# Postponing weight-conversion steps at the start of row 1, and two reorderings around it, in a fused attention and mixer kernel

## The chip, the cores and the metric

The kernel runs on one core of one Trainium2 chip. The metric is the device time of one launch in microseconds (us). A core has five instruction streams that matter here: TensorE (PE, matrix multiplication, with its weight loads as PEld), VectorE (DVE), ScalarE (ACT), GpSimd (POOL) and SyncE (SP, which here only issues DMA transfers). The streams run side by side and wait for each other through semaphores.

## The reference

The first half is attention over 8 batch rows, 8 heads, 576 tokens and a head width of 64, in which scores more than `tau` below the row's maximum are dropped. The second half is one mixer block on the joined heads.

```python
scores = scale * np.matmul(q, k.transpose(0, 1, 3, 2))
thresh = np.max(scores, axis=-1, keepdims=True) - tau
scores = np.where(scores >= thresh, scores, -1000000000.0)
attn = softmax(scores)
x = np.matmul(attn, v)               # then heads side by side: (8, 576, 512)
h = np.maximum(xt @ w_tok1, 0.0) @ w_tok2         # over tokens, xt = x transposed
u = x + h.transpose(0, 2, 1)
h2 = np.maximum(u @ w_ch1, 0.0) @ w_ch2           # over channels, 512 -> 1536 -> 512
return (u + h2)
```

(`softmax` stands for the reference's lines that subtract the maximum, take the exponential and divide by the sum.) The four mixer weights reach the kernel as 64-bit integers that hold float64 bit patterns. The kernel turns them into float32 itself, and that is what this change is about.

## The kernel before

**Units.** Attention is cut into 144 units, 18 to each batch row: two pairs of heads at a time, and a tile of 128 query rows. The main loop (L648) goes over `u`; row 0 is units 0 to 17, row 1 is units 18 to 35. One turn of the loop issues, for unit u, `scores(u)` (TensorE, L306), then the row maximum `mx` (VectorE, L311) and `bias` (GpSimd, L312), and `weigh(u)` on ScalarE: `e` from the scores (L321), then the exponential (L328). It also issues `norm(u-1)` (GpSimd, L339), and for unit w = u-2 the transposition of `e`. Row 0 transposes on TensorE in thirds (`turn`, L357, copied out at L359). Later rows use a VectorE block transpose (`turn_blocks`, L369), and after every third unit that is followed by 16 transfers `eT<-T` issued by SyncE (L378). Every three units `values` (L413, L418) multiplies by v, and the result is copied into `xT`: at L425 by VectorE in row 0, at L423 by ScalarE later. In row 0 these copies are first put in the queue `copies`, which the loop empties a little later. A unit of row 0 in which `values` runs is called a visit: units 5, 8, 11, 14 and 17.

Each engine takes its instructions in the order in which this loop issues them. From row 1 on the score tiles have two PSUM buffers and one unit fills both, so `scores(u+1)` on TensorE has to wait until L321 of `weigh(u)` has read them.

**Filling.** The mixer's work for a finished row is a list `todo` of steps with costs in us. `fill(share)` takes steps from it against a quota per unit. In row 1 a unit calls it with 0.4 ahead of `turn_blocks` and three times with 0.2 inside `weigh`. For row 0 the list is made in unit 20: the token layers (L456, L466, with their VectorE additions L470), then for each group of 256 tokens twelve steps `ch1` of the first channel layer (L509, copied out on ScalarE at L510) and eight steps `ch2` of the second (L530): two halves of 128 tokens (t) by four parts of the weights (part). These steps take their PSUM tile from `ps_mm`, which has two buffers.

**Weight conversion.** The weights are 31 pieces, from 0 to 30. Raw pieces are loaded into a ring of four slots by SyncE (L186). The conversion is a chain of numbered steps k, three for a piece i: k = 3i + part.

- Part 0: GpSimd finishes piece i-1 (L225), SyncE issues the load of piece i+3 into the slot that this frees, and VectorE does L211 for piece i.
- Part 1: ScalarE does L201 for piece i+1, which is the first instruction to read that piece's load, and VectorE does L213 for piece i.
- Part 2: ScalarE does L203 for piece i+1, and VectorE does L217 for piece i.

`weight(n)` issues the next n steps, `weight_to(x)` goes on to step x, and `need(i)` issues whatever is missing for piece i. In row 0 the loop keeps to int(2.25 (u-1)) steps by the end of unit u, so 36 at the end of unit 17. In row 1 a unit has three places for steps, called slots here: slot 1 after `norm`, slot 2 after `turn_blocks` and ahead of `weigh`, slot 3 at the end, after `weigh`. In units 18 and 19, in which row 0's last units still wait to be transposed, `turns_left` is true: slot 1 is empty, `weigh` comes early in the unit, and slot 2 stands after it.

Of the kernel before, what the change touches and what calls it, by code (L numbers as in the profile page):

```python
# [9 lines left out]
F32 = mybir.dt.float32  # L10
# [7 lines left out]
P = 128  # L18
# [3 lines left out]
def kernel(  # L22
# [38 lines left out]
    NCC = DM // P  # L61
# [16 lines left out]
    ps_mm = None  # L78
# [118 lines left out]
    def on_scalar(i, part):  # L197
        if wide(i):
            lo, hi, h2 = raws[i]
            if part == 0:  # L200
                nc.scalar.activation(out=lo.bitcast(I32), in_=lo, func=AF.Copy, scale=2.0**-29)  # L201
            else:
                nc.scalar.activation(out=h2, in_=hi.bitcast(F32), func=AF.Abs)  # L203
# [17 lines left out]
    def on_gpsimd(i):  # L221
        if i >= 0:
            dst = pieces[i][0]
            if wide(i):
                nc.gpsimd.tensor_tensor(out=dst.bitcast(I32), in0=dst.bitcast(I32), in1=raws.pop(i)[0].bitcast(I32), op=ALU.add)  # L225
            else:
                nc.gpsimd.tensor_copy(out=dst, in_=raws.pop(i))
# [5 lines left out]
    def weight(n):  # L233

        nonlocal steps_done
        for k in range(steps_done, min(steps_done + n, 3 * len(pieces) + 1)):
            i, part = divmod(k, 3)
            if part == 0:
                on_gpsimd(i - 1)
                if i:  # L240
                    load_piece(i - 1 + NRAW)
            else:
                on_scalar(i + 1, part - 1)
            on_vector(i, part)
            steps_done = k + 1

    def weight_to(x):

        weight(max(int(x) - steps_done, 0))

    def need(i):

        weight(3 * i + 4 - steps_done)
# [27 lines left out]
    def in_blocks(b):  # L281
        return b > 0
# [32 lines left out]
    def weigh(u):  # L315
        sc, bias = st.pop(u)
        rs = small.tile([P, 2], F32, tag="rs", name=f"rs_{u}")
        e = work.tile([P, 2 * S], F32, tag="e", bufs=3, name=f"e_{u}")
        for h in range(2):
            eh = e[:, S * h : S * h + S].rearrange("p (f x) -> p f x", f=2)  # L320
            nc.scalar.activation(out=eh, in_=sc[h][:, :, 0:HS], func=AF.Prelu, bias=bias[:, h : h + 1], scale=SCALE, alpha=STEEP)  # L321
        st[u] = e, rs

        if b_now:
            fill(0.2)
        for h in range(2):
            eh = e[:, S * h : S * h + S]
            nc.scalar.activation(out=eh, in_=eh, func=AF.Exp, bias=ntau, accum_out=rs[:, h : h + 1])  # L328
            if b_now:
                fill(0.2)  # L330
# [153 lines left out]
    def channel_mlp(b, uT, i):  # L484

        s = {}
        n = min(GR, 2 * S - GR * i)
        nt = n // P

        def turn_u():  # L490

            us, ut = s["us"], s["ut"]
            nc.vector.transpose(
                out=us[:, 0:nt].rearrange("q n a (c d) -> q c (n a) d", c=NCC),
                in_=uT[:, :, GR * i : GR * i + n].rearrange("q c (m r) -> q c m r", r=32),
            )

            def move(a, k):
                nc.sync.dma_start(out=ut[32 * a : 32 * a + 32, 0:nt, k, :], in_=us[32 * k : 32 * k + 32, 0:nt, a, :])

            moves.extend([lambda a=a, k=k: move(a, k) for a in range(4) for k in range(4)])

        def ch1(j):
            need(7 + j)
            if j == 0:
                s["g"] = work.tile([P, NJ, GR], F32, tag="g", bufs=1, name=f"g_{b}_{i}")
            ps = ps_mm.tile([P, GR], F32, tag="mm", name=f"c1_{b}_{i}_{j}")[:, 0:n]
            for c in range(NCC):
                nc.tensor.matmul(ps, lhsT=wc1[:, j, c, :], rhs=uT[:, c, GR * i : GR * i + n], start=(c == 0), stop=(c == NCC - 1))  # L509
            nc.scalar.activation(out=s["g"][:, j, 0:n], in_=ps, func=AF.Relu)  # L510
            if j == 1:
                s["us"] = work.tile([P, GR // P, 4, NCC * 32], F32, tag="us", bufs=1, name=f"us_{b}_{i}")
                if b:
                    s["ut"] = work.tile([P, GR // P, 4, NCC * 32], F32, tag="ut", bufs=1, name=f"ut_{b}_{i}")
                    turn_u()

        def ch2(t, part):
            need(7 + NJ + 3 * part + 2)
            t0 = GR * i + P * t
            if part == 0:  # L520
                s["ps"] = ps_mm.tile([P, NCC, P], F32, tag="mm", name=f"c2_{b}_{i}_{t}")
            ps = s["ps"]
            flat = ps.rearrange("q c d -> q (c d)")
            if part == 0 and not b:
                for c in range(NCC):
                    nc.tensor.matmul(
                        ps[:, c, :], lhsT=uT[:, c, t0 : t0 + P], rhs=ident, is_transpose=True, start=(c == 0), stop=False, skip_group_check=True
                    )
            for j in range(3 * part, 3 * part + 3):
                nc.tensor.matmul(  # L530
                    flat,
                    lhsT=s["g"][:, j, P * t : P * t + P],
                    rhs=wc2[:, j, :],
                    start=(j == 0 and b > 0),
                    stop=(j == NJ - 1),
                    skip_group_check=True,
                )
            if part == 3:
                o = s["us"][:, t].rearrange("q a x -> q (a x)")
                if b:  # L540
                    move_u()
                    nc.vector.tensor_add(  # L542
                        out=o.rearrange("q (c k d) -> q c k d", c=NCC, k=4),
                        in0=ps.rearrange("q c (k d) -> q c k d", k=4),
                        in1=s["ut"][:, t].rearrange("q k (c d) -> q c k d", c=NCC),
                    )
                else:
                    nc.vector.tensor_copy(out=o, in_=flat)
                nc.sync.dma_start(out=out[b : b + 2].rearrange("b s d -> (b s) d")[t0 : t0 + P, :], in_=o)

        def ch2_last(half):

            t0 = GR * i
            w = DM // 2
            ps = ps_mm.tile([P, w], F32, tag="mm", name=f"c2_{b}_{i}_h{half}")
            for j in range(NJ):
                nc.tensor.matmul(  # L557
                    ps, lhsT=s["g"][:, j, 0:P], rhs=wc2[:, j, w * half : w * half + w], start=(j == 0), stop=(j == NJ - 1)
                )
            if half == 0:  # L560
                move_u()
            o = s["us"][:, half].rearrange("q a x -> q (a x)")[:, 0:w]
            cs = slice(NCC // 2 * half, NCC // 2 * half + NCC // 2)
            nc.vector.tensor_add(
                out=o.rearrange("q (c k d) -> q c k d", c=NCC // 2, k=4),
                in0=ps.rearrange("q (c k d) -> q c k d", c=NCC // 2, k=4),
                in1=s["ut"][:, 0].rearrange("q k (c d) -> q c k d", c=NCC)[:, cs],
            )
            nc.sync.dma_start(out=out[b : b + 2].rearrange("b s d -> (b s) d")[t0 : t0 + P, w * half : w * half + w], in_=o)

        if b == B - 2 and n == P:
            return [(0.0067 * n, lambda j=j: ch1(j)) for j in range(NJ)] + [(5.2, lambda half=half: ch2_last(half)) for half in range(2)]
        return [(0.0067 * n, lambda j=j: ch1(j)) for j in range(NJ)] + [
            (2.6 if part or b else 3.0, lambda t=t, part=part: ch2(t, part)) for t in range(nt) for part in range(4)
        ]

    def move_u():
        while moves:
            moves.popleft()()
# [68 lines left out]
    for u in range(len(units) + LAG + 4):  # L648
        on = u < len(units)
        if u == UB:  # L650
            late.close()
            ps_mm = ctx.enter_context(tc.tile_pool(name="ps_mm", bufs=2, space=bass.MemoryType.PSUM))
        if on:
            b_now, p0, t = units[u]
# [6 lines left out]
        last = False  # L661
        visit = False
        if due and not in_blocks(due[0][1]):
            visit = due[0][0] <= u
            last = values_due(u)
# [6 lines left out]
        turns_left = b_now and back and not in_blocks(units[w][0])  # L672
        if b_now:
            if turns_left:
                weigh(u)
            else:
                weight(2)
        else:


            weight_to(2.25 * (u - (1 if visit else 1.5)))
            if visit:
                weigh(u)
        while copies:
            copies.popleft()()
        if last and u < UB:
# [15 lines left out]
        if back and in_blocks(wb):  # L702
            turn_blocks(w)
        if b_now:
            weight(4 if turns_left else 2)
        if turns_left:
            fill(0.6)
        elif on and (b_now or not visit):
# [62 lines left out]
```

## Time and profile before

| | |
|---|---|
| time, median of 3 | 1351.52 us (1350.7 to 1352.07) |
| span of the profiled run | 1349.9 us |
| PE busy, 0 to 100 us | 81.77 of 100.00 us |
| PE busy, 100 to 190 us | 78.78 of 90.00 us |
| PE busy, 190 us to the end | 1146.08 of 1159.90 us |
| VectorE busy, 0 to 100 and 100 to 190 us | 74.95 and 76.72 us |

Row 0's scores run to about 90 us, the conversion ends at about 188 us, and the rest is almost solid TensorE work. In a list of the timeline a line gives the start, the duration, the engine, the line of code, the operation with its output and input, how many instructions are merged into it, and in brackets how long the engine had been idle before it and what it waited for.

### The profile page before, as it was taken

How to read it: one execution, taken by the hardware profiler on the slowest of the kernel's cores; microseconds unless marked ns; L12 is line 12 of the kernel's file. 1: busy time of each engine (PE TensorE's matmuls, PEld its weight loads, DVE VectorE, ACT ScalarE, POOL GpSimd, SP SyncE). 2: the span in 40 equal slices, each digit the busy share in tenths (PEclk: the TensorE clock that was granted, in tenths of full speed). 3: DMA queues.
4: the chain of work that ended last, by engine and by line, in shares of the span. 5: the costliest groups of instructions: out<-in, count | busy, mean ns of one | idle time of the engine just before them, and what ended most of it. 6: DMA issues, size and time to landing. Idle time of an engine off the chain costs nothing.

```text
span 1349.9 us, 17890 instructions
## 1 busy us (share of the span) xinstructions
PE 1306.6 (97%) x6186; PEld 817.1 (61%) x6186; DVE 592.2 (44%) x1026; ACT 585.1 (43%) x1299; POOL 352.5 (26%) x683
## 2 busy tenths in 40 slices
PE   7888899999999999999999999999999999999999
PEld 5565556547474666655665567565656566575677
DVE  6878874445443435434334445434443454201000
ACT  6777654444445435443434444354333454120110
POOL 4565652222222213222222222222221222100000
PEclk8998999999999999999999999999999999999999
DMA  5535764535353544543345435535443453400000
GB/s 123 120 87 127 199 168 97 127 94 136 83 133 89 114 109 96 126 109 88 86 107 125 98 85 123 125 82 115 109 102 83 114 118 79 112 22 17 23 24 32
DMA packets 296746, 135.31 MB, mean 100 GB/s; under 512 B 204816, under 2 KB 289552, under 8 KB 296656
## 3 DMA queue, kind: packets, MB, share of 16 engines
q1 hardware_dynamic: 168944, 118.27, 34.4%
q10 hardware_dynamic: 127712, 15.90, 7.4%
q8 instruction: 49, 0.80, 0.3%
q14 instruction: 41, 0.34, 0.1%
HBM read 43.25 MB, written 9.44 MB: 39 GB/s over the span
## 4 chain that ended last, share of the span: by engine, by line
PE 86%; DVE 6%; DMA 3%; ACT 2%; SPq 1%; issue 1%; POOL 1%; ACTq 0%; DVEq 0%; POOLq 0%
PE c L530 26%; PE c L509 26%; PE sc L306 11%; PE pv L418 9%; PE t L456 5%; PE t L466 4%; PE pv L413 3%; DVE mx L311 2%; PE tx L449 1%; DMA lk<-in_k_dram 1%; ACT e L321 1%; SPq L378 1%; PE c_h L557 1%; DVE T L369 1%; DVE high L211 1%
## 5 line engine op out<-in xcount | busy, mean ns | idle before, releaser
L509 PE MATMUL c<-xT,wc 128*128 128x256 f32 (+1 forms) x1920 | 400.1, 362 | 0.1
L311 DVE TENSOR_REDUCE mx<-sc 128x1 f32<-128x576 f32 x288 | 204.4, 750 | 444.3 <-PE sc L306 443.2
L530 PE MATMUL c<-wc,g 128*128 128x512 f32 x840 | 379.0, 597 | 0.0
L509 PEld LDWEIGHTS c<-xT,wc 128*128 128x128 f32 x1920 | 334.9, 191 | 69.3 <-issue 29.7
L312 POOL TENSOR_SCALAR bias<-mx,toff 128x1 f32<-128x1 f32 x288 | 81.1, 282 | 775.6 <-DVE mx L311 722.7
L321 ACT ACTIVATE e<-sc,bias 128x576 f32<-128x576 f32 x288 | 199.8, 739 | 182.5 <-POOL bias L312 176.7
L530 PEld LDWEIGHTS c<-wc,g 128*128 128x128 f32 x840 | 154.7, 190 | 176.1 <-issue 172.4
L328 ACT ACTIVATE e<-e,ntau 128x576 f32<-128x576 f32 x288 | 221.1, 771 | 0.0
L339 POOL TENSOR_SCALAR e<-e,rr 128x576 f32<-128x576 f32 x288 | 214.3, 756 | 14.8 <-ACT g L510 2.6
L510 ACT ACTIVATE g<-c 128x256 f32<-128x256 f32 (+1 forms) x240 | 86.7, 361 | 296.5 <-PE c L509 283.4
L306 PE MATMUL sc<-kT,qT 64*128 64x288 f32 (+1 forms) x1280 | 190.3, 433 | 6.9 <-ACT e L321 5.9
L369 DVE STREAM_TRANSPOSE T<-e 128x1152 f32<-128x1152 f32 x126 | 171.9, 1364 | 5.5 <-DMA eT<-T 2.9
L306 PEld LDWEIGHTS sc<-kT,qT 64*128 64x128 f32 (+1 forms) x1280 | 105.2, 178 | 92.2 <-issue 57.2
L418 PE MATMUL pv<-eT,lv 128*64 128x384 f32 (+1 forms) x1024 | 136.8, 408 | 0.0
L418 PEld LDWEIGHTS pv<-eT,lv 128*64 128x64 f32 x1024 | 76.9, 138 | 49.9 <-issue 42.1
L423 ACT COPY xT<-pv 128x384 f32<-128x384 f32 (+1 forms) x56 | 21.0, 400 | 164.6 <-PE pv L418 159.5
L466 PE MATMUL t<-w,a 128*128 128x288 f32 x256 | 75.2, 421 | 8.2 <-DVE xT L470 4.8
L542 DVE TENSOR_TENSOR us<-c,ut 128x512 f32<-128x512 f32 x26 | 17.9, 690 | 137.5 <-PE c L530 122.7
L456 PE MATMUL t<-x_sb,w 128*128 128x512 f32 (+1 forms) x180 | 72.4, 549 | 0.0
L466 PEld LDWEIGHTS t<-w,a 128*128 128x128 f32 x256 | 45.9, 192 | 30.2 <-issue 10.5
L470 DVE TENSOR_TENSOR xT<-xT,t 128x288 f32<-128x288 f32 x64 | 28.3, 446 | 70.6 <-PE t L466 69.9
L328 ACT ACTIVATION_READ_ACCUMULATOR e<-e,ntau 128x1 f32 x288 | 56.7, 197 | 0.0
(51 smaller groups left out, 571.2 us busy)
## 6 DMA issues: line engine op xcount, KB each, us to landing
eT<-T SPq DMA_DIRECT2D x672, 108.0 KB, 2.3
scratch<-in_moe_w_ch_dram SPq DMA_DIRECT2D x24, 512.0 KB, 3.7
lv<-in_v_dram SPq DMA_DIRECT2D x32, 288.0 KB, 3.5
out_dram<-us SPq DMA_DIRECT2D x35, 256.0 KB, 2.2
lk<-in_k_dram ACTq DMA_DIRECT2D x109, 72.0 KB, 2.7
lq<-in_q_dram ACTq DMA_DIRECT2D x106, 72.0 KB, 2.3
ut<-us SPq DMA_DIRECT2D x192, 32.0 KB, 1.9
lk<-in_k_dram SPq DMA_DIRECT2D x19, 72.0 KB, 3.2
```

What stands on the lines that cost most here:

```text
L306: nc.tensor.matmul(sc[h][rows, f, 0:HS], lhsT=qT[r, cols], rhs=kT[r, HS * f : HS * f + HS], start=True, stop=True)
L311: nc.vector.tensor_reduce(out=mx[:, c], in_=sc[h][:, :, 0:HS], axis=AX.XY, op=ALU.max)
L321: nc.scalar.activation(out=eh, in_=sc[h][:, :, 0:HS], func=AF.Prelu, bias=bias[:, h : h + 1], scale=SCALE, alpha=STEEP)
L328: nc.scalar.activation(out=eh, in_=eh, func=AF.Exp, bias=ntau, accum_out=rs[:, h : h + 1])
L339: nc.gpsimd.tensor_scalar(out=eh, in0=eh, scalar1=rr[:, h : h + 1], scalar2=1.0, op0=ALU.mult, op1=ALU.mult)
L369: nc.vector.transpose(out=T[:, :, place, :].rearrange("p a (c x) -> p c a x", c=NK), in_=e.rearrange("p (c a x) -> p c a x", c=NK, a=4))
L418: nc.tensor.matmul(to[r], lhsT=lv[:, j, :], rhs=e[j], start=False, stop=(c == NI - 1), skip_group_check=True)
L456: nc.tensor.matmul(to, lhsT=w1[:, t, P * m : P * m + P], rhs=x_sb[:, t, cols], start=(t == 0), stop=(t == NT - 1))
L466: nc.tensor.matmul(to, lhsT=a[:, m, P * c : P * c + P], rhs=w2[:, m, HS * f : HS * f + HS], start=(m == 0), stop=(m == NTK - 1))
L509: nc.tensor.matmul(ps, lhsT=wc1[:, j, c, :], rhs=uT[:, c, GR * i : GR * i + n], start=(c == 0), stop=(c == NCC - 1))
L510: nc.scalar.activation(out=s["g"][:, j, 0:n], in_=ps, func=AF.Relu)
L530: nc.tensor.matmul(flat, lhsT=s["g"][:, j, P * t : P * t + P], rhs=wc2[:, j, :], start=(j == 0 and b > 0), stop=(j == NJ - 1), skip_group_ ...
```

## The change

Three edits. In units 18 and 19, slot 2 issues no steps where it issued four, so the chain is eight steps further back from there on; nothing is left out, and the later slots go on with two steps each until step 93 is done. The eight `ch2` steps of the first token group are taken by part of the weights first (part 0 of both halves, then part 1 of both, and so on), so that the later weights are called for later; both `ps_mm` buffers are then held through the group, so each half keeps its own tile. In the visits of row 0, the steps no longer stand between `norm` and the copies, but at the end of the unit, where the call of `weight_to` that is already there picks them up.

```diff
             if part == 0:
-                s["ps"] = ps_mm.tile([P, NCC, P], F32, tag="mm", name=f"c2_{b}_{i}_{t}")
-            ps = s["ps"]
+                s[t] = ps_mm.tile([P, NCC, P], F32, tag="mm", name=f"c2_{b}_{i}_{t}")
+            ps = s[t]
...
+        last = [(t, part) for t in range(nt) for part in range(4)]
+        if b == 0 and i == 0:
+            last.sort(key=lambda x: x[1])
         return [(0.0067 * n, lambda j=j: ch1(j)) for j in range(NJ)] + [
-            (2.6 if part or b else 3.0, lambda t=t, part=part: ch2(t, part)) for t in range(nt) for part in range(4)
+            (2.6 if part or b else 3.0, lambda t=t, part=part: ch2(t, part)) for t, part in last
         ]
...
-            weight_to(2.25 * (u - (1 if visit else 1.5)))
             if visit:
                 weigh(u)
+            else:
+                weight_to(2.25 * (u - 1.5))
...
         if b_now:
-            weight(4 if turns_left else 2)
+            weight(0 if turns_left else 2)
```

## The prediction

> **What bounds the kernel now.** I read PE's busy row and PEclk in the page's 40 slices first.
>
> ```profile
> PE   7888899999999999999999999999999999999999
> DVE  6878874445443435434334445434443454201000
> PEclk8998999999999999999999999999999999999999
> ```
>
> A slice is 33.7 us. From the sixth on PE is full; its idle time lies in the first five, where VectorE is as busy. After 190 us PE is busy 1146.08 of 1159.90 us, so a shift reached there is carried to the end. What counts is PE's idle time before that. Next, PE's timeline in units 19 and 20:
>
> ```profile
> 106.10 0.82 PE L357 MATMUL tr<-ident,e 128*128 128x128 f32 x6
> 111.28 0.90 PE L357 MATMUL tr<-ident,e 128*128 128x128 f32 x3 [4.37 <-DVE eT L359]
> 112.11 2.29 PE L306 MATMUL sc<-kT,qT 64*128 64x288 f32 x8
> 114.34 1.55 PE L413 MATMUL pv<-eT,vl 128*64 128x384 f32 x4
> 115.67 3.74 PE L418 MATMUL pv<-eT,lv 128*64 128x384 f32 x16
> 119.34 3.18 PE L466 MATMUL t<-w,a 128*128 128x288 f32 x12
> ```
>
> PE stands 4.37 us for a VectorE copy and is slow afterwards: scores take 2.29 us, against 1.24 at 98.53. VectorE meanwhile:
>
> ```profile
> 104.17 0.60 DVE L211 TENSOR_SCALAR high<-high 128x512 f32<-128x512 f32 x1
> ...
> 106.87 0.74 DVE L211 TENSOR_SCALAR high<-high 128x512 f32<-128x512 f32 x1 [0.92 <-ACT high L203]
> ...
> 108.72 1.42 DVE L311 TENSOR_REDUCE mx<-sc 128x1 f32<-128x576 f32 x2
> ...
> 110.69 0.54 DVE L359 COPY eT<-tr 128x384 f32<-128x384 f32 x1
> ```
>
> Unit 19's scores were ready at 105.1, but six steps of unit 18 stand ahead of its maximum and the copy. That is what the change attacks. Last, SyncE's and ScalarE's timelines, for where else the steps are held:
>
> ```profile
> 140.53 0.33 SPq L186 DMA_DIRECT2D scratch<-in_moe_w_ch_dram  x1
> 140.90 10.55 SPq L378 DMA_DIRECT2D eT<-T  x16
> 151.57 16.15 SPq L186 DMA_DIRECT2D scratch<-in_moe_w_ch_dram  x6
> ```
>
> ```profile
> 146.32 0.70 ACT L203 ACTIVATE high<-scratch 128x512 f32<-128x512 f32 x1
> 146.93 1.35 ACT L321 ACTIVATE e<-sc,bias 128x576 f32<-128x576 f32 x2
> ...
> 155.41 0.69 ACT L201 ACTIVATE scratch<-scratch 128x512 int32<-128x512 uint32 x1 [5.08 <-DMA scratch<-in_moe_w_ch_dram]
> ```
>
> The sixteen `eT<-T` of unit 22 hold SyncE for 10.55 us. The load behind them starts at 151.57, and L201 has waited for it 5.08 us. That wait lies behind unit 23's L321, in slot 3.
>
> [...] after the 4.37 us, granted clock 0.50 from 112 to 116. [...] So a waiting L201 holds every L321 behind it; the lines above agree. [...] L211 takes 0.41 us alone and 1.52 at 131.90 beside L225.
>
> **Visits (edit 3).** In units 8 and 17 the steps delay the copies that PE waits for. In unit 17 they run from 95.06 to 97.0, while pv ended at 95.54; PE starts at 97.68 and could at about 96.1: 1.5 us won. In unit 8 0.76 us of steps make 0.6. In units 5, 11 and 14 the steps now run inside VectorE's wait for pv (0.99, 2.31 and 1.68 us idle) and cost nothing; moved behind the copies they push the next maximum by steps less idle time there: about 0.3, 0.4 (part of 0.86 hidden) and 0.1. Sum **-1.3 us** (minus is earlier).
>
> **Eight steps fewer (edit 1), units 18 to 20.** Two steps remain of six. VectorE is through at 105.2, the maximum ends at 106.6, the addition L470 (0.44), `norm`'s pair (0.3) and the copy (0.54) bring PE's next transposition to 107.8: idle 0.9 instead of 4.37, so -3.5. The clock stays up: the scores save 1.05, pv 1.55 (3.45 instead of 5.0). L466 starts at about 113.1 instead of 119.34: **-6.2**.
>
> **Units 20 to 22.** Six steps per unit as before, but in another phase: slot 1 now holds L213 and L217 (1.13 us) instead of L211 and L213 (0.85), and slot 3 holds L211 behind a L203 that follows `weigh`. Against that, L211 and L213 meet L225 less often. I take **+1.0**; between -2 and +2 is possible.
>
> **The wait that moves.** Count steps. Unit 22 starts at step 60 before, at 52 after, as 36 + 2 + 2 + 6 + 6. Its `eT<-T` stand between slots 1 and 2. The first load behind them is issued before with step 63 (piece 24) and read by L201 in step 70: unit 23's slot 3, behind `weigh(23)`. After, it is issued with step 54 (piece 21) and read in step 61: slot 2, **ahead of** `weigh(23)`. Queued behind that L201 are unit 23's L321 and exponentials; `scores(24)` waits for L321, and all PE work behind it too. From the end of the T transposition of unit 22 (140.0 in before's time): 0.1 + 10.55 + 3.65 for landing (151.57 to 155.2) + 0.6 for L201 + 0.7 for the first L321 = 15.6 us. PE's work ahead of `scores(24)` ends at 149.4, or 9.4 after that transposition. So it idles about 6.4 us[...] and runs at half clock, 2.3 us lost (scores 1.05, first layers 1.25). The old wait at this place, 1.82 us at 159.48, goes: **+6.9**.
>
> Unit 25 has the same pattern: step 72 loads piece 27 behind the sixteen transfers, and step 79 reads it in unit 26's slot 2. Before, it was step 81 and step 88 in slot 3, where ScalarE waits 6.20 us but PE only 0.94. PE's work between T and `scores(27)` runs from 165.6 to 174.1, or 8.5 us; the chain is 15.6 again; with half clock for about 2 us, less 0.94 and some waiting that `scores` had inside its rows: **+7.7**. Unit 28's sixteen are followed by no load.
>
> **The second layer's order (edit 2).** Steps reach 88 by the end of unit 27 and 94 in unit 28. By weights, part 2 (needs 85) comes around unit 30, part 3 (94) after it: `need` adds nothing, and the copies L548 hide behind PE. The eight late steps load VectorE in unit 28: **+0.5**, at most 2.
>
> Sum: -1.3 - 6.2 + 1.0 + 6.9 + 7.7 + 0.5 = +8.6; 1351.5 + 8.6 = **1360 us**.
>
> **Rivals.**
> - Faster: the waits that move cost PE no more than the old ones, because a load comes sooner or PE has work left. For it: PE bridged 5.08 and 6.20 us on ScalarE with 1.82 and 0.94 idle. Against: these stood behind L321. -1.3 - 6.2 + 1.0 + 0.5 = -6.0: 1345.5 us.
> - About the same: only one of the two moved waits costs PE its full size; -6.0 + 6.9 = +0.9: 1352.4 us.
> - Slower still: the clock stays halved for 6 us, as from 111 to 117, and unit 28 costs 2 us: 8.6 + 2 x 1.6 + 1.5 = 13.3: 1365 us.
>
> **Chances.** Forecast 0.55, slower still 0.08, the same 0.12, faster 0.25. The limit of 0.2% is 2.7 us, and the case around 1352.4 spreads over it a little on both sides: faster 0.26, same 0.09, slower 0.65. The range, 1344.5 to 1364, takes in the faster rival and the unknown half-clock times, and leaves out the slowest case and a stray tail.
>
> **What would show it.** Right: PE's 4.37 us before L357 shrinks to about 1; L201 waits some 8 us for its load twice, each time just ahead of a L321; PE's `scores` wait over 5 us for L321 near 150 and 175; half clock behind both. Wrong: L201's long waits still follow the exponentials, or `scores` never waits over 3 us there; then the gain of 6 us stands.

## The result, and the profile after

The changed kernel takes 1362.53 us, the median of 6 runs (1360.37 to 1364.71), against 1352.44 for the kernel before in the same session. The ratio is 1.0075, with a 95% interval of 1.006 to 1.0089: 10.1 us slower. The profiled run has a span of 1360.1 us.

The busy row of PE and the granted clock, from the page of the changed kernel:

```profile
PE   7888879999999999999999999999999999999999
...
PEclk8999889999999999999999999999999999999999
```

A slice is 34.0 us. Against the kernel before, the fourth slice has won a tenth of clock, the fifth (136 to 170 us) has lost one, and the sixth (170 to 204 us) has lost a tenth of clock and two of busy time. PE's timeline says where. A number in brackets is the time that PE stood still ahead of the line, and what it waited for:

```profile
106.90 0.55 PE L357 MATMUL tr<-ident,e 128*128 128x128 f32 x3 [1.83 <-DVE eT L359]
107.38 1.24 PE L306 MATMUL sc<-kT,qT 64*128 64x288 f32 x8
...
112.20 3.18 PE L466 MATMUL t<-w,a 128*128 128x288 f32 x12
...
136.48 1.24 PE L306 MATMUL sc<-kT,qT 64*128 64x288 f32 x8
137.65 5.45 PE L509 MATMUL c<-xT,wc 128*128 128x256 f32 x24
149.30 2.92 PE L306 MATMUL sc<-kT,qT 64*128 64x288 f32 x8 [6.20 <-ACT e L321]
152.14 5.83 PE L509 MATMUL c<-xT,wc 128*128 128x256 f32 x16
...
161.28 1.24 PE L306 MATMUL sc<-kT,qT 64*128 64x288 f32 x8
...
182.05 2.92 PE L306 MATMUL sc<-kT,qT 64*128 64x288 f32 x8 [6.97 <-ACT e L321]
...
195.57 1.24 PE L306 MATMUL sc<-kT,qT 64*128 64x288 f32 x8
```

The same stretch in the kernel before, from unit 23's scores on:

```profile
142.84 1.24 PE L306 MATMUL sc<-kT,qT 64*128 64x288 f32 x8
144.01 5.45 PE L509 MATMUL c<-xT,wc 128*128 128x256 f32 x24
149.39 1.24 PE L306 MATMUL sc<-kT,qT 64*128 64x288 f32 x8
150.56 3.72 PE L509 MATMUL c<-xT,wc 128*128 128x256 f32 x16
...
159.48 1.86 PE L306 MATMUL sc<-kT,qT 64*128 64x288 f32 x8 [1.82 <-ACT e L321]
...
185.45 1.87 PE L306 MATMUL sc<-kT,qT 64*128 64x288 f32 x8 [0.94 <-ACT e L321]
```

Unit 19 has won what the change was made for. The wait of 4.37 us is 1.83, the scores behind it take 1.24 us at a granted clock of 1.00 (107 to 110 us), and L466 starts at 112.20 instead of 119.34. At unit 23's scores (136.48, before 142.84) the kernel is still 6.4 us ahead. Then unit 24's scores wait 6.20 us for L321 and unit 27's 6.97. Unit 28's start at 195.57, where before they started at 185.45: 10.1 us behind. After that the distance hardly changes: unit 40's scores start at 281.41 and 272.14, 9.3 us apart, and the last unit's at 1158.78 and 1148.55, 10.2 us apart.

ScalarE's timeline shows what L321 waits for, and SyncE's why the load is late:

```profile
147.97 0.65 ACT L201 ACTIVATE scratch<-scratch 128x512 int32<-128x512 uint32 x1 [7.90 <-DMA scratch<-in_moe_w_ch_dram]
148.52 1.36 ACT L321 ACTIVATE e<-sc,bias 128x576 f32<-128x576 f32 x2
...
180.72 0.65 ACT L201 ACTIVATE scratch<-scratch 128x512 int32<-128x512 uint32 x1 [8.54 <-DMA scratch<-in_moe_w_ch_dram]
181.28 1.35 ACT L321 ACTIVATE e<-sc,bias 128x576 f32<-128x576 f32 x2
```

```profile
133.52 10.43 SPq L378 DMA_DIRECT2D eT<-T  x16
144.06 17.10 SPq L186 DMA_DIRECT2D scratch<-in_moe_w_ch_dram  x6
166.67 10.31 SPq L378 DMA_DIRECT2D eT<-T  x16
177.10 1.01 SPq L186 DMA_DIRECT2D scratch<-in_moe_w_ch_dram  x2
```

Both times the load is issued when the sixteen transfers are out (144.06, 177.10), lands 3.82 and 3.54 us later, and L201 and at once L321 follow it. The waiting L201 holds L321: unit 23's `bias` starts at 139.50 and takes 0.27 us, and L321, which needs it, starts at 148.52. In the kernel before, unit 24's starts at 152.83 and its L321 at 158.69, behind the L201 that waited 5.08 us and the steps after it. Before, the L201 that waited stood behind the exponentials; here it stands directly ahead of L321, so the order in the queue is what has changed.

One rival has to be looked at here. At the first place the chain of waits names GpSimd's L225 as what released the load: it ends at 144.05, and the transfers are out at 143.95. But this L225 belongs to step 60. The one that frees the slot for this load belongs to step 54 and runs at 133.28 for 1.28 us, and in e4_load_ahead below, where nothing stands ahead of it on SyncE, the load of step 54 is issued at 135.01. So it is the transfers that hold it. At the second place the chain itself runs through all sixteen of them.

### The profile page after: what moved, and what is told of

It is laid out like the page before. It is cut to its first block, busy times and chain, and to the rows that moved or that the text cites. A ratio compares the mean times of both kernels' runs of the same rounds, so it can differ in the third digit from the quotient of the medians.

```text
span 1360.1 us, 17887 instructions
## 1 busy us (share of the span) xinstructions
PE 1309.0 (96%) x6186; PEld 818.6 (60%) x6186; DVE 587.5 (43%) x1026; ACT 585.6 (43%) x1299; POOL 353.5 (26%) x683
## 4 chain that ended last, share of the span: by engine, by line
PE 86%; DVE 5%; ACT 3%; DMA 2%; SPq 1%; POOL 1%; issue 1%; ACTq 0%; DVEq 0%; POOLq 0%
PE c L509 26%; PE c L530 26%; PE sc L306 11%; PE pv L418 9%; PE t L456 5%; PE t L466 4%; PE pv L413 3%; DVE mx L311 2%; SPq L378 1%; PE tx L449 1%; DMA lk<-in_k_dram 1%; ACT e L321 1%; PE c_h L557 1%; PE tr L357 1%; ACT e L328 1%
## 5 line engine op out<-in xcount | busy, mean ns | idle before, releaser
L509 PE MATMUL c<-xT,wc 128*128 128x256 f32 (+1 forms) x1920 | 402.7, 364 | 0.1
L509 PEld LDWEIGHTS c<-xT,wc 128*128 128x128 f32 x1920 | 336.5, 192 | 70.7 <-issue 29.7
L321 ACT ACTIVATE e<-sc,bias 128x576 f32<-128x576 f32 x288 | 200.0, 740 | 186.4 <-POOL bias L312 183.9
L418 PE MATMUL pv<-eT,lv 128*64 128x384 f32 (+1 forms) x1024 | 136.3, 406 | 0.0
L418 PEld LDWEIGHTS pv<-eT,lv 128*64 128x64 f32 x1024 | 76.2, 137 | 48.4 <-issue 38.9
L466 PE MATMUL t<-w,a 128*128 128x288 f32 x256 | 74.9, 418 | 8.6 <-DVE xT L470 5.2
L466 PEld LDWEIGHTS t<-w,a 128*128 128x128 f32 x256 | 45.3, 190 | 30.8 <-issue 10.5
```

The lines of the kernel that those rows point to most:

```text
L418: nc.tensor.matmul(to[r], lhsT=lv[:, j, :], rhs=e[j], start=False, stop=(c == NI - 1), skip_group_check=True)
L466: nc.tensor.matmul(to, lhsT=a[:, m, P * c : P * c + P], rhs=w2[:, m, HS * f : HS * f + HS], start=(m == 0), stop=(m == NTK - 1))
```

## The experiments

The question was whether the loss comes from the place of those reads in the count of six steps per unit, or from something else that the change does: the larger backlog itself, the new order of the second layer, or the steps moved in the visits. All ratios are to the kernel before, run beside it on the same chip.

### The three edits one at a time

```diff
# e1_steps_only: the kernel before, with
-            weight(4 if turns_left else 2)
+            weight(0 if turns_left else 2)
# e2_order_only: the kernel before, with a tile for each half, s[t], and
+            last.sort(key=lambda x: x[1])
# e3_visits_only: the kernel before, with
-            weight_to(2.25 * (u - (1 if visit else 1.5)))
             if visit:
                 weigh(u)
+            else:
+                weight_to(2.25 * (u - 1.5))
```

> Only the eight steps fewer; copies and second layer as before. Theory (the first load behind the sixteen transfers is now read ahead of weigh): both long waits of scores for L321 stand as in the changed kernel, 6 to 7 us each, and the visits' gain of 1 to 2 us is missing: about 1364 us, ratio 1.008 to 1.010. Rival (the second layer's order, holding both PSUM buffers, is what costs): the gain of units 18 to 20 remains alone, about 1346 us, ratio 0.995.

Measured: 1363.76 us, ratio 1.0088 (1.0074 to 1.0103). The scores wait 5.39 and 7.02 us for L321. So this edit alone makes the loss; what the two others add or save is within the intervals.

> Only the second layer by weights. Theory: the order moves no wait, within 1 us of before (1351.5 to 1353.5). Rival (the order is what costs): 1357 us or more.

Measured: 1352.66 us, ratio 1.0003 (0.9995 to 1.0011): no difference. Beside the backlog the order may have a use: e1_steps_only, without it, shows two waits in PE's timeline that the changed kernel doesn't have, for GpSimd's last step on the late pieces, 1.7 us in all. In the medians this can't be told from noise:

```profile
202.37 1.13 PE L530 MATMUL c<-wc,g 128*128 128x512 f32 x2 [0.37 <-POOL wc L225]
204.80 1.12 PE L530 MATMUL c<-wc,g 128*128 128x512 f32 x2 [1.30 <-POOL wc L225]
```

> Only the steps behind the copies in the visits. Theory: PE's wait for the copies L425 in units 8 and 17 shrinks from 1.25 and 1.66 us to under 0.5; 1 to 2 us faster than before: about 1351. Rival (the steps behind the copies delay the next maximum and cost more than they save): 1353 to 1356.

Measured: 1351.21 us, ratio 0.9992 (0.9984 to 1.0): about 1 us, at the edge of what the interval can tell. Its PE timeline in units 8 and 17 has the wait that was to shrink, from 1.25 and 1.66 us to 0.34 both times:

```profile
46.62 0.92 PE L357 MATMUL tr<-ident,e 128*128 128x128 f32 x6 [0.34 <-DVE xT L425]
...
96.14 0.92 PE L357 MATMUL tr<-ident,e 128*128 128x128 f32 x6 [0.34 <-DVE xT L425]
```

### The size of the backlog against the place in the count

If backlog costs, fewer steps left out must cost less. If the place costs, three steps in slot 2 (a backlog of two) must do what none does (a backlog of eight), for in both the first load behind the transfers is issued in a unit's slot 2 (with step 60 and with step 54, both multiples of six) and read in the next unit's slot 2, ahead of `weigh`.

```diff
# the changed kernel, with n = 3, 2 or 1
-            weight(0 if turns_left else 2)
+            weight(n if turns_left else 2)
```

> The changed kernel with three steps instead of none in slot 2 of units 18 and 19: only two steps of backlog instead of eight, but the same place in the count of six. Step 60 issues the first load behind the sixteen transfers, step 67 reads it in unit 23's slot 2, ahead of weigh. Theory (place counts): both waits of scores for L321 stand, over 5 us each, and most of the gain at unit 19 is gone: 1360 to 1368 us. Rival (backlog counts): within 2 us of before, 1350 to 1354.

> The same with two steps instead of none: four steps of backlog. The first load behind the transfers is step 60 in slot 3, read by step 67 in unit 23's slot 3, behind weigh. Theory: no wait of scores for L321 over 3 us; half the gain at unit 19: 1345 to 1351 us. Rival (backlog counts): between the two kernels, about 1357.

> The same with one step instead of none: six steps of backlog, exactly one unit, so every step keeps the slot that it had before. First load behind the transfers step 57, read by step 64 in unit 23's slot 3, behind weigh. Theory: waits of scores for L321 as before (1 to 3 us), most of the gain at unit 19: 1344 to 1349 us. Rival (backlog counts): about 1360.

| steps in slot 2 | backlog | us | ratio (95%) |
|---|---|---|---|
| 4, the kernel before | 0 | 1351.99 | |
| 3 | 2 | 1364.45 | 1.0093 (1.0076 to 1.0109) |
| 2 | 4 | 1351.7 | 0.9998 (0.9988 to 1.0007) |
| 1 | 6 | 1350.85 | 0.9994 (0.9983 to 1.0005) |
| 0, the changed kernel | 8 | 1362.53 | 1.0075 (1.006 to 1.0089) |

A backlog of two costs as much as one of eight, within the intervals, and backlogs of four and six cost nothing that can be told from zero. The list of waits, between 98 and 215 us, says the same. First three steps, then one step; the columns are who waited for whom, us in total, times, and the longest:

```profile
PE sc L306 <- ACT e L321: 12.7, 3, 6.9
PE tr L357 <- DVE eT L359: 5.1, 2, 4.3
```

```profile
PE sc L306 <- ACT e L321: 5.2, 3, 2.6
PE tr L357 <- DVE eT L359: 3.2, 2, 2.6
```

But the expectation for two steps and for one held only in the waits. The times were to fall to 1344 to 1351, and fell by nothing that can be told from zero. With one step the lead is 6.6 us at unit 24's scores (142.76, before 149.39), 5.0 at unit 25's (154.52, before 159.48), and only 1.5 at unit 28's (183.97, before 185.45). Over this stretch ScalarE waits 6.93, 6.19 and 3.08 us for loads, where before it waited 5.08, 0.62 and 6.20, and PE waits 2.11 and 2.63 us for L321, where before it waited 1.82 and 0.94. Behind the first of these waits PE is also slow: unit 25's scores take 2.50 us, against 1.24 for unit 24's, and the 24 matmuls of L509 behind them 6.45, against 5.45 from 137.38 on. So part of what unit 19 wins is taken back by waits for the same loads, even in a harmless place.

### Moving the load out from behind the transfers

Three ways were tried. In the first, slot 2 goes ahead of `turn_blocks` where the sixteen transfers follow it:

```diff
# e4_load_ahead: the changed kernel, with
+        ahead = b_now and back and in_blocks(wb) and wt % GU == GU - 1
+        if ahead:
+            weight(2)
         if back and in_blocks(wb):
             turn_blocks(w)
-        if b_now:
+        if b_now and not ahead:
             weight(0 if turns_left else 2)
```

> The changed kernel, with slot 2 ahead of turn_blocks in the units whose turn_blocks is followed by sixteen transfers, so that the load of step 54 and of step 72 is issued before them. Nothing else moves. Theory: the two waits of scores for L321 (6.20 and 6.97 us) fall under 2 us and the gains stay: 1345 to 1349 us, ratio 0.994 to 0.998. Rival (eight steps of backlog cost wherever the load stands, because VectorE is full until unit 28): stays above 1358.

Measured: 1357.11 us, ratio 1.0031 (1.0022 to 1.0041): over half of the loss is gone, and the gain of the changed kernel's early units doesn't come through. The profiled execution was the fastest of nine, 1353.92 us, so its trace may show less than the median lost. In it, the long waits of the scores fell to 1.55 and 0.31 us, but the loads in slot 3 now stand behind the transfers. L201 waits 5.87 us in unit 23 and 6.28 in unit 26, then 2.20 ahead of unit 27's L321, and unit 28's scores wait 2.83. Later the transposed tiles of unit 28 come late to PE, and matmuls slow down again (4.47 us for L418, against 2.75):

```profile
204.93 0.87 PE L413 MATMUL pv<-eT,vl 128*64 128x384 f32 x4 [2.10 <-DMA eT<-T]
205.59 4.47 PE L418 MATMUL pv<-eT,lv 128*64 128x384 f32 x16
```

In the second, GpSimd issues the loads behind the L225 that frees their slot:

```diff
# e7_pool_loads: the changed kernel, with
-        nc.sync.dma_start(out=like(raw, dst), in_=src)
+        (nc.sync if i < NRAW else nc.gpsimd).dma_start(out=like(raw, dst), in_=src)
# e7_pool_loads_one: with one step in slot 2 of units 18 and 19 besides
```

> The changed kernel, with the raw loads from the fifth piece on issued by GpSimd, right behind the L225 that frees their slot, instead of by SyncE. They no longer stand behind the sixteen transfers. Theory (SyncE's queue holds the load, that holds L201, that holds weigh): L201's two waits of 7.90 and 8.54 us fall under 2 us, scores no longer waits over 2 us for L321, and the gain of units 18 to 20 is kept: 1343 to 1348 us. Rival (eight steps of backlog cost, or the transfers' own traffic delays the load): above 1355. GpSimd's issuing may cost something of its own on bias.

> As e7_pool_loads, with one step in slot 2 of units 18 and 19, so six steps of backlog. Theory: with the loads off SyncE the place in the count matters little any more, so within 2 us of e7_pool_loads: 1343 to 1348 us. Rival (place counts by itself): over 4 us apart from it.

Measured: 1363.29 us (1.0076, 1.0057 to 1.0094) and 1363.14 us (1.0066, 1.004 to 1.0091). Both lie in the range of the first run's rival, above 1355, and not at the expected 1343 to 1348. The place in the count no longer matters, as expected: the two are alike. The waits of L201 fell from 7.90 and 8.54 to at most 3.31 us in e7_pool_loads, and the scores wait 0.58 for L321. From unit 18's scores to unit 28's this run falls 5.4 us behind the kernel before, and the changed kernel 12.0. What it lost came mainly from two places. First, unit 18's scores start at 101.43, against 96.68 in the changed kernel, so row 0 is 4.7 us slower with the loads on GpSimd (two traces of the same row 0, before and e2_order_only, are 2.2 us apart there); which of its waits make that was not followed up. Second, the sixteen transfers now run beside the loads and land late. In the chain of waits of e7_pool_loads one of them lands after 9.11 us and another after 5.96, where in the changed kernel the sixteen from 133.5 to 143.4 take 2.3 in the median. PE stands for the last of them:

```profile
141.79 9.11 DMA eT<-T
...
153.47 5.96 DMA eT<-T
```

```profile
159.78 1.55 PE L413 MATMUL pv<-eT,vl 128*64 128x384 f32 x4 [6.66 <-DMA eT<-T]
```

The late landings come while GpSimd issues loads, at 140.24, 142.44, 148.91, 151.36 and 157.06. But the loads have also changed to another kind of queue, as the page's list of queues shows (packets, MB, and their share of the 16 engines' span); the kernel before has no such queue:

```profile
q0 software_dynamic: 3696, 13.47, 3.3%
```

No run separates the loads beside the transfers from this. What is shown is that SyncE's queue was not only a hindrance: with the loads behind them there, the transfers of the changed kernel landed in 2.3 us in the median.

In the third, the transfers are split, eight ahead of slot 2 and eight behind it:

```diff
# e8_split_none and, with one step in slot 2 of units 18 and 19, e8_split_one
-            for a in range(4):
+            def go(a):
                 for i in range(4):
                     nc.sync.dma_start(...)
+            go(0)
+            go(1)
+            rest.extend([lambda: go(2), lambda: go(3)])
...
             weight(0 if turns_left else 2)
+        while rest:
+            rest.popleft()()
```

> The changed kernel with the sixteen transfers in two halves, eight ahead of slot 2 and eight behind it, so the load in slot 2 (steps 54 and 72) stands behind eight, some 5 us earlier. Theory: the waits of L201 (7.90 and 8.54) shrink by about 5 us each and scores' waits by about as much; against that the transfers' second half lands later: 1350 to 1355 us. Rival (backlog): above 1358.

> As e8_split_none, with one step in slot 2 of units 18 and 19. First load behind the half is step 57 in slot 2, read by step 64 behind weigh(23). Theory: the waits left in e5_one_step (6.93, 6.19 and 3.08 us on L201, 2.11 and 2.63 on PE) shrink, and the 5 us that were won at unit 20 are kept to the end: 1345 to 1348 us. Rival (what was given back there has another cause): 1350 to 1352 as e5_one_step.

Measured: 1355.5 us (1.002, 1.001 to 1.003) and 1351.16 us (0.9986, 0.9978 to 0.9994). With no steps in slot 2 three quarters of the loss are gone. Its profiled execution was the slowest of twenty, 1360.96 us, so its waits can't be set beside the median: in it L201 waits 4.34 and 3.92 us, and the scores 2.65 and 2.38.

With one step it is the only complete version whose interval lies wholly below the kernel before, by 0.14%. But 1351.16 is in the range of its rival, that the return of the gain has another cause (1350 to 1352), and not at the expected 1345 to 1348. In the trace waits have moved more than gone: PE waits 3.12 us for the transfers in unit 24, half of which are now issued later, and ScalarE 6.86 us for a load in unit 27. So this run doesn't settle what takes the gain back.

### Without the late loads

The last run leaves out what all the others only moved: the raw loads of pieces 21 to 30. All steps still run, on what the slots hold, so the weights from piece 21 on are not the right ones.

```diff
# e9_late_loads_out: the changed kernel, with
-        nc.sync.dma_start(out=like(raw, dst), in_=src)
+        if i < 21:
+            nc.sync.dma_start(out=like(raw, dst), in_=src)
```

> The changed kernel without the raw loads of pieces 21 to 30: those from the first load behind unit 22's sixteen transfers on. All conversion steps still run, on what the ring's slots hold from before, so the weights of the channel layers from piece 21 on are not converted from their own data. Theory (the whole loss is these loads: their wait, or their traffic beside the transfers): no wait of scores for L321 over 1 us, the gain of units 18 to 20 is kept: 1342 to 1347 us, ratio 0.992 to 0.996. Rival (eight steps of backlog cost on VectorE and ScalarE by themselves): 1350 or more.

Measured: 1345.47 us, ratio 0.9946 (0.9929 to 0.9962). The waits of PE from 98 to 215 us (each line number is one higher, so L307 is the scores and L322 is L321):

```profile
PE t L467 <- DVE xT L471: 3.4, 2, 2.7
PE tr L358 <- DVE eT L360: 2.4, 2, 1.8
PE pv L414 <- issue: 2.1, 1, 2.1
PE sc L307 <- ACT e L322: 0.4, 1, 0.4
```

The same eight steps are postponed, VectorE, ScalarE and GpSimd run every one of them, and the time is 7.3 us under the kernel before. The loss of the changed kernel goes with the late loads: with their wait, or with their traffic, which this run takes away together. That the backlog costs nothing at all is not shown. The 7.3 us also hold waits of the kernel before that are gone here (PE's 1.82 and 0.94), and the kernel before was not run without these loads. A small cost is in the trace: from unit 21's scores (121.33) to unit 23's (139.71) the lead over the kernel before falls from 4.80 to 3.13 us, and in the changed kernel from 7.14 to 6.36. That the return of the gain with one or two steps comes from the loads as well is likely from the waits above, but no run leaves them out there.

## Why the prediction was right

The forecast was 1360 us and slower, in a range of 1344.5 to 1364; 1362.53 was measured, near the upper end. Its steps, in its own order:

- **Visits.** -1.3 us was forecast. e3_visits_only gives a ratio of 0.9992, or -1.1 us of 1352. Both waits in units 8 and 17 shrank to 0.34. In the trace of the changed kernel unit 18's scores are 1.85 us earlier (96.68, before 98.53), but single traces differ by as much at this place: in e2_order_only, whose row 0 is that of the kernel before, they start at 100.73.
- **Units 18 to 20.** With the visits, L466 was to start 7.5 us sooner; it started 7.14 sooner. That this is so close is in part luck: 1.85 of it was there at unit 18's scores, so units 18 to 20 won 5.3 us and not 6.2. The wait at unit 19 is 1.83 and not 0.9: one of the two steps left, L213, took 1.40 us (103.02) and not 0.43 beside GpSimd's L225 (102.63 to 104.14), so the maximum began at 104.35. The scores and pv (the product with v, L413 and L418) ran at full clock as forecast, 1.24 and 3.45 us at a granted clock of 1.00 from 107 to 113.
- **Units 20 to 22.** +1.0 was forecast; the lead went from 7.14 to 6.36, +0.8.
- **The wait that moves.** Both places were right, and the sizes nearly. The scores' waits were to be about 6.4 and near 7; they were 6.20 and 6.97. (For the first, the prediction's own terms, 15.6 less 9.4, make 6.2.) The lead of 6.36 became a lag of 1.80 at unit 25's scores (161.28 against 159.48): 8.2 us, and 6.9 was forecast. By unit 28 the lag was 10.12: 8.3 us, and 7.7 was forecast.
- **Unit 28.** +0.5 was forecast. From unit 28's scores to unit 40's the lag fell from 10.1 to 9.3, and at the last unit it was 10.2, so next to nothing was added.

The term of the sum that was most too small is the half clock behind the first wait. The forecast took 2.3 us for it: 1.05 on the scores and 1.25 on the first layer. The windows of the changed kernel show why it was more; the columns are the stretch, the busy time and instructions of PE, PEld, DVE, ACT and POOL, the granted clock, the DMA share and GB/s:

```profile
149.00:152.00 3.00, 2.70 (x8) 1.80 (x8) 0.00 (x0) 3.00 (x9) 0.00 (x0) 0.50 0.95 312
152.00:155.00 3.00, 3.00 (x8) 2.32 (x8) 2.42 (x7) 1.57 (x3) 0.91 (x3) 0.50 0.04 8
155.00:158.00 3.00, 3.00 (x13) 2.26 (x13) 2.97 (x4) 2.04 (x4) 3.00 (x3) 0.76 0.01 3
```

The clock is at 0.50 from the first matmul at 149.3 to beyond 156 (0.50 from 155 to 156 as well), over 6 us. The scores take 2.92 instead of 1.24, and the sixteen matmuls of L509 take 5.83 instead of 3.72 as at 150.56 before: 1.68 + 2.11 = 3.8 us. That is 1.5 more than was put down. That +8.6 and this 1.5 make just the measured +10.1 is luck: the other terms missed too, by +0.4 up to L466, -0.2 in units 20 to 22, -0.2 in the first wait itself, +0.6 at the second wait and -0.4 from unit 28 on, and these nearly cancel. The prediction had the longer half clock, as seen from 111 to 117 us before, in its slower rival, and should have taken it for the likeliest. Its 2.3 us were the author's estimate, beside the half clock of the trace before as cited from 112 to 116 only. That trace as well shows 0.50 in each microsecond from 111 to 117 and 0.67 in the next. That a half clock would follow an idle time of 6.4 us at all was its estimate too, with the one case of 4.37 us behind it.

Of the rivals, the faster one lost because the moved loads do cost PE more than the old ones did. Its 1345.5 us and the 1345.47 of e9_late_loads_out agree by chance: that rival kept the old waits of PE, 1.82 and 0.94 us, and started from 1351.5, while e9_late_loads_out has no such wait and was run beside a kernel before of 1352.78. The rival in which only one wait counts is ruled out by the two long waits in the trace.

## What to carry to other kernels

When a stream of background steps is shifted in a hand-written order, count where each waiting instruction lands against the instruction that feeds the bounding engine. Here a wait behind it was cheap (5.08 and 6.20 us on ScalarE cost PE 1.82 and 0.94), and a wait ahead of it was not (7.90 us cost PE 6.20 and over 6 us at a clock of 0.50 besides), and one step decided (1351.7 us with two steps in slot 2, 1364.45 with three). Look at the count modulo the steps of one round, not at how many steps were moved: a backlog of two was as bad as one of eight, four and six did no harm. And before another queue is given a late transfer, see which transfers will then run beside it (one of 9.11 us here, against a median of 2.3).

## What was not expected

- Moving the loads to GpSimd's queue (e7_pool_loads) brought every wait for them to 3.31 us or less and gained nothing in the whole: one `eT<-T`, with a median of 2.3 us to landing, took 9.11 us beside them, and PE waited 6.66 us for the last.
- With one step in slot 2 PE's wait at unit 19 was down to 2.58 us and unit 24's scores were 6.6 us ahead, and 5.1 of that were gone by unit 28's scores, while ScalarE waited for loads again.
- The clock stayed at 0.50 for over 6 us of unbroken matmul work after an idle time of 6.20 us, and about as long after one of 4.37 us before, but only about 3 us after one of 3.02 us (138.4 to 141.7 before). Nor does the length of the idle time alone tell whether the matmuls behind it are slow. In the kernel before, four matmuls of L466 took 1.24 us at a clock of 1.00 (105.03) and 2.29 at 0.50 (138.41). In e8_split_none the scores took 2.85 us after an idle time of 2.65, where they take 1.24 at a clock of 1.00, and in e5_one_step four of L466 took 1.24 us after one of 3.04:

```profile
147.94 2.85 PE L306 MATMUL sc<-kT,qT 64*128 64x288 f32 x8 [2.65 <-ACT e L321]
```

```profile
133.32 1.24 PE L466 MATMUL t<-w,a 128*128 128x288 f32 x4 [3.04 <-DVE xT L470]
```

What decides it, these runs don't show.
